# Weight conversion without clamp and magnitude, range checks moved to later blocks, in an attention and two-layer MoE kernel

## Chip, cores, metric

The kernel runs on one core of one Trainium2 chip. The metric is the time on the device in microseconds (us), the median of several executions; lower is better.

## What is computed

Three layers follow each other: a linear attention with a decay for each key row, a dense layer with a squared ReLU, and a layer of eight experts whose outputs are weighed by a matrix that is normalised eight times by rows and columns (Sinkhorn).

```python
# q, k, v, f_logit: (4, 8, 768, 48)
f = 1.0 / (1.0 + np.exp(-f_logit))
for t in range(S):
    state = f[:, :, t, :, None] * state + np.einsum('bhd,bhe->bhde', k[:, :, t], v[:, :, t])
    y[:, :, t] = np.einsum('bhd,bhde->bhe', q[:, :, t], state)

# x: (3072, 384), w_in: (384, 2048), w_out: (2048, 384)
r = np.maximum(x @ w_in, 0.0)
x = (r * r) @ w_out

# w_gate: (384, 8), w1: (8, 384, 1024), w2: (8, 1024, 384); P is N x 8
for e in range(E):
    h = np.maximum(x @ w1[e], 0.0)
    out += P[:, e:e + 1] * (h @ w2[e])
```

`w_in` and `w_out` are float64; the kernel reads their eight bytes as an int64 and makes a float32 of them itself.

## The kernel before

**Stages.** The 3072 tokens are eight blocks of 384 (NB = 8), each of three chunks of 128 (c = 0 to 23, three to a block). The dense layer goes block by block, and in each block over 16 slices of the hidden width (NF = 16). Step i = 16 * block + slice has a first product `e1` (`products_in`, L713 in block 0, L717 later), a ReLU `r` (L722) and a square `sq` (L725) on ScalarE, from block 1 on a rounding `hi` on ScalarE (L729) and a rest `lo` on VectorE (L733), and a second product `e2` (`m_out`, L742 in block 0, L746 later), two steps behind. From block 1 on each product is three matmuls with float32r parts. After the eight blocks come the experts (L983 and L1045).

**Attention of the next block** runs between the steps of the dense layer. For a chunk there are on TensorE `kt` (the transposed keys, L474), `sc` (scores, L459 or L453), `ds` (the state's increment, L499 or L492) and `mix` (the output, L537 and L546, from chunk 6 on L553); on VectorE two scans (`scanr` L400 to 402, `scanf` L407), the products `mulk` and `mulq` (L412, L416, later on GpSimd), the causal mask (L469, L464), the state (L507) and its decayed copy (L429). From chunk 6 on, a `mix` writes into the two PSUM banks of `e1`, so it waits for the ReLU of the step before it; the outputs leave by a ScalarE copy `yh` and a VectorE rest `yl` (L597, L595), and the next `e1` of that bank waits for them. When the three chunks of a block are done, `spread` (L603) moves rows inside the block's input by six DMAs; the block's first `e1` waits for these.

**Weight conversion.** For slice n, `ldw` loads 768 int64 values in each of 128 partitions. Class `F64` makes float32 of them: the magnitude of the high word (ScalarE, L1362), the low word scaled (ScalarE, L1365), a clamp of the magnitude to the float32 range (VectorE, L1370), the exponent and mantissa bits shifted (VectorE, L1375), the sign put in (VectorE, L1379), and the sum of both words (GpSimd, L1383). The result `R[n]` is what block 0 multiplies with. For block 1 and later it is split: `cvh` (ScalarE, L335) and `cvl` (VectorE, L338). Four raw buffers serve the 16 loads, so load n + 4 waits for the sum of n.

**Operands for the experts.** When a block's output `x2t` is there (L753), `xbs` (L875), `xbh` (ScalarE, L882) and `xbl` (L886) make sums of its rows, and `xbo` (L891) writes each of 15 operands to DRAM. Two buffers of the pool `rawp` hold them, and later the raw expert weights.

**The order.** All instructions are steps of a class `Plan`: engine, assumed duration, due time (in steps of the dense layer), needs, and an earliest start in microseconds. `Plan.order` lists the steps engine by engine in the order of an assumed schedule; each engine then runs its own list strictly in that order. The set `soft` holds steps that yield to others, the set `port` steps on VectorE and GpSimd that are not to overlap. SyncE's list is the order of all DMA issues, each assumed to take 0.48 us. `keep_warm` (L284) fills idle stretches of TensorE's assumed schedule in the first part with matmuls of no use.

```python
def load(self, name, kb, due, fn, needs=(), n=1, start=0.6, rate=350.0):
    self.add(name + ("issue",), "sp", 0.48 * n, due, fn, needs, start=start)
    self.add(name, "dma", kb / rate, due, lambda: None, [name + ("issue",)], lag=1.2)
```

**Ranges.** A flag says whether a general path has to run instead: `in_range` takes the least decay of all chunks (`minf`) and compares it with a bound. Weights outside the float32 range are clamped.

Of the kernel before, what the change touches and what calls it, by code (L numbers as in the profile page):

```python
# [28 lines left out]
NCH = B * NCB  # L29
# [50 lines left out]
class Plan:  # L80
# [15 lines left out]
    def add(self, name, eng, dur, due, fn, needs=(), lag=0.0, start=0.0):  # L96
        assert name not in self.steps, name
        self.steps[name] = (eng, dur, due, fn, [n for n in needs if n is not None], lag, start)

    def load(self, name, kb, due, fn, needs=(), n=1, start=0.6, rate=350.0):  # L100
        self.add(name + ("issue",), "sp", 0.48 * n, due, fn, needs, start=start)
        self.add(name, "dma", kb / rate, due, lambda: None, [name + ("issue",)], lag=1.2)

    def order(self):
# [75 lines left out]
def body(tc, fkq, v, wm, wa, wc, gate, seqs, out):  # L180
# [49 lines left out]
    def if_(ok, name):  # L230
        return name if ok else None
# [93 lines left out]
    def cv_abs(n):  # L325
        cvt[n] = cvp.tile([128, KD, TB // 2 + 1], F32, tag="t", name="cv_t")
        R[n] = wb.tile([128, WCOL], F32, tag=f"b{n}", name="r")
        F64(nc, cvt[n][:, :, 0:TB // 2], raws[n], R[n]).magnitude()

    def cv_total(n):  # L330
        F64(nc, cvt[n][:, :, 0:TB // 2], raws[n], R[n]).total(R[n])

    def cv_hi(n):
        new_w(n)
# [3 lines left out]
        dve.tensor_tensor(out=W[n][1], in0=R[n], in1=W[n][0].bitcast(F32), op=ALU.subtract)  # L338

    for n in range(NF):  # L340
        part = lambda m, n=n: getattr(F64(nc, cvt[n][:, :, 0:TB // 2], raws[n], R[n]), m)()
# [8 lines left out]
        plan.off_port |= {("cvb", n, 0), ("cvb", n, 1)}  # L350
# [248 lines left out]
    def spread(blk):  # L599
        X = x1[blk].bitcast(F32)  # L600
        for j in range(2):
            for k in range(KD):
                sp.dma_start(out=X[64 * j + DH:64 * j + 64, :, k, :], in_=X[64 * j + 16 * k:64 * j + 16 * k + 16, :, NP - 1, :])  # L603

    moved = []
    for c in range(NCH):
# [80 lines left out]
        else:  # L687
            at("yl", "none", 0, 3, lambda c: None, [("yh", c)])
        if q == CPB - 1 and blk:
            add(("sprd", blk), "sp", 3.0, g + to(3, 0.5), lambda blk=blk: spread(blk), [("yl", c - i) for i in range(CPB)], lag=2.2)  # L690

    def close_left():
        left.close()
# [194 lines left out]
    def xb_out(j, o):  # L888
        p, c = divmod(j, NB // NGRP)
        n = xb_at(j, o)  # L890
        sp.dma_start(out=xd[p, o][:, :, c * 128:(c + 1) * 128], in_=xb[j][:, n:n + 2])  # L891
# [197 lines left out]
    users += [("xb", j, [("xbo", j, o) for o in ROW_OPS]) for j in range(NB - 1)]  # L1089
    for g in range(NSTEP):  # L1090
        users += [("wa", g, [("w2lo", g, 0), ("w2lo", g, 1), ("wsum", g, 5)]), ("wc", g, [("w2lo", g, 2), ("w2lo", g, "c")])]
    slot_of = {}
    for n in range(2, len(users)):
        prev = users[n - 1]
        slot_of[users[n][:2]] = users[n - 2][2] + ([] if n == 2 else [("ld" + prev[0], prev[1], "issue")])

    for j in range(NB):
# [12 lines left out]
        for n, o in enumerate(ROW_OPS):  # L1110
            src = list(src0)
            m = SUMS.index(o) if o in ROW_SUM else 0
            if o in ROW_SUM and m >= (2 if mine else 1):
                src.append(("xbl", j, SUMS[m - (2 if mine else 1)]))
            if o in ROW_SUM and not mine:
                src.append(("xbl", j, ROW_OPS[n - 1]) if n else None)
            if o == 10:
                src += [("xbs", j, 2, len(ROW_SUM[2]) // 2 - 1)]
            if o == 5:
                src += [("xbs", j, 10, 0)]  # L1120
            for k in range(len(ROW_SUM.get(o, ())) // 2):
# [5 lines left out]
            add(("xbo", j, o, "issue"), "sp", 0.48, due(n) + 0.2, lambda j=j, o=o: xb_out(j, o), [("xbl", j, o)])  # L1127
# [221 lines left out]
class F64:  # L1349

    def __init__(self, nc, t, raw, flat=None):
        self.nc, self.t, self.flat = nc, t, flat
        self.high = raw.bitcast(I32).rearrange("p (n two) -> p n two", two=2)[:, :, 1]
        self.word = raw.bitcast(U32).rearrange("p (n two) -> p n two", two=2)[:, :, 0]

    def like(self, a):
        return a.rearrange("p (a b) -> p a b", a=KD) if self.flat is not None else a

    def magnitude(self):
        self.nc.scalar.activation(out=self.t, in_=self.like(self.high.bitcast(F32)), func=ACTF.Abs)  # L1362

    def low(self):
        self.nc.scalar.activation(out=self.word.bitcast(I32), in_=self.word, func=ACTF.Copy, scale=2.0 ** -29)  # L1365

    def clamp(self):
        dve, t = self.nc.vector, self.t
        out = t if self.flat is None else self.like(self.flat)
        dve.tensor_scalar(out=out, in0=t, scalar1=F64_LOW, scalar2=F64_HIGH, op0=ALU.max, op1=ALU.min)  # L1370

    def fields(self):
        dve, ti = self.nc.vector, self.t.bitcast(I32)
        src = ti if self.flat is None else self.like(self.flat.bitcast(I32))
        dve.tensor_scalar(out=ti, in0=src, scalar1=0x07FFFFFF, scalar2=3, op0=ALU.bitwise_and, op1=ALU.logical_shift_left)  # L1375

    def sign(self):
        dve, ti = self.nc.vector, self.t.bitcast(I32)
# [263 lines left out]
```

## Time and profile before

| | |
|---|---|
| runs | 1983.05, 1983.74, 1985.0 us; median 1983.74 |
| profiled execution | 1984.72 us, of which 1982.7 us are the span from the first to the last instruction |
| TensorE busy | 1964.8 us, 99% of the span |
| VectorE, ScalarE, GpSimd busy | 1399.0, 908.5, 972.4 us |
| mean granted TensorE clock | 0.998 |

The profile's page lists busy time by engine and by source line. Its other views are a timeline of one engine (with the idle time before an instruction, and what ended it), a table of busy time by stretches, the chain of work that ended last (followed back from the end), and groups of instructions by line. In those, a float32 matmul counts twice (two passes), so a slice's product of three such matmuls stands as x6, and one of nine float32r matmuls as x9.

### The profile page before, as it was taken

How to read it: one execution, taken by the hardware profiler on the slowest of the kernel's cores; microseconds unless marked ns; L12 is line 12 of the kernel's file. 1: busy time of each engine (PE TensorE's matmuls, PEld its weight loads, DVE VectorE, ACT ScalarE, POOL GpSimd, SP SyncE). 2: the span in 40 equal slices, each digit the busy share in tenths (PEclk: the TensorE clock that was granted, in tenths of full speed). 3: DMA queues.
4: the chain of work that ended last, by engine and by line, in shares of the span. 5: the costliest groups of instructions: out<-in, count | busy, mean ns of one | idle time of the engine just before them, and what ended most of it. 6: DMA issues, size and time to landing. Idle time of an engine off the chain costs nothing.

```text
span 1982.7 us, 29656 instructions
## 1 busy us (share of the span) xinstructions
PE 1964.8 (99%) x10921; PEld 1665.1 (84%) x10921; DVE 1399.0 (71%) x2314; ACT 908.5 (46%) x1643; POOL 972.4 (49%) x915
## 2 busy tenths in 40 slices
PE   8999999999999999999999999999999999999998
PEld 6699999999988888888888888888888888888887
DVE  8987666752577777666777777676677777766676
ACT  6665555655644443333444443433444444333342
POOL 2520111100245667776665556646666556666661
PEclk9999999999999999999999999999999999999999
DMA  7524343425202111121111114411111011111101
GB/s 267 179 77 115 106 111 100 111 70 188 79 33 66 49 53 58 59 67 48 57 33 48 33 49 161 142 32 57 33 55 49 32 48 33 56 40 48 40 24 50
DMA packets 102322, 146.61 MB, mean 74 GB/s; under 512 B 23608, under 2 KB 71320, under 8 KB 102168
## 3 DMA queue, kind: packets, MB, share of 16 engines
q1 hardware_dynamic: 102168, 144.63, 23.2%
q8 instruction: 88, 1.44, 0.3%
q14 instruction: 66, 0.54, 0.1%
HBM read 115.42 MB, written 21.14 MB: 69 GB/s over the span
## 4 chain that ended last, share of the span: by engine, by line
PE 94%; DVE 4%; issue 1%; DMA 1%; ACT 0%; SPq 0%; DVEq 0%; ACTq 0%
PE o L1045 40%; PE e L983 33%; PE a L746 8%; PE e L717 8%; PE a L742 1%; PE e L713 1%; PE y L553 1%; PE lg L761 1%; DVE sg L400 1%; PE pp L492 0%; PE pp L453 0%; PE ktr L474 0%; DVE QP L464 0%; DVE cv_t L1375 0%; DVE r L1370 0%
## 5 line engine op out<-in xcount | busy, mean ns | idle before, releaser
L1045 PE MATMUL o<-h,w 128*128 128x512 f32 x3456 | 790.7, 389 | 0.0
L1045 PEld LDWEIGHTS o<-h,w 128*128 128x128 f32 x3456 | 648.3, 188 | 135.0
L983 PE MATMUL e<-x,w 128*128 128x512 f32 x2304 | 536.2, 390 | 0.2 <-DVE vt L1010 0.2
L983 PEld LDWEIGHTS e<-x,w 128*128 128x128 f32 x2304 | 430.0, 188 | 94.5 <-DVE vt L1006 2.4
L1081 POOL TENSOR_TENSOR acc<-acc,sc 128x512 f32<-128x512 f32 x252 | 388.0, 1548 | 129.8 <-DVE sc L1072 126.6
L1072 DVE TENSOR_TENSOR sc<-o,pb 128x512 f32<-128x512 f32 x261 | 179.3, 687 | 213.6 <-PE o L1045 209.0
L934 ACT CAST w<-rawa 128x640 fp32r<-128x640 f32 x128 | 89.8, 726 | 285.3 <-DMA rawa<-in_wa_dram 142.7
L1010 DVE TENSOR_TENSOR v<-v,e 128x512 f32<-128x512 f32 x256 | 174.8, 683 | 64.5 <-PE e L983 57.8
L717 PE MATMUL e<-x,w 128*128 128x384 f32 x1008 | 193.5, 337 | 2.0 <-DMA x<-x 1.8
L934 ACT CAST w<-rawc 128x640 fp32r<-128x640 f32 (+1 forms) x128 | 97.2, 782 | 209.1 <-PE o L1045 157.9
L938 DVE TENSOR_TENSOR w<-rawa,w 128x640 fp32r<-128x640 f32 x128 | 152.6, 1211 | 57.2 <-ACT w L934 57.1
L1029 POOL TENSOR_TENSOR h<-vt,h 128x512 fp32r<-128x512 f32 x64 | 83.5, 1305 | 199.6 <-ACT vt L1024 197.4
L717 PEld LDWEIGHTS e<-x,w 128*128 128x128 f32 x1008 | 175.8, 188 | 3.8 <-ACT xb L882 2.0
L746 PE MATMUL a<-hi,w 128*128 128x384 f32 x672 | 173.9, 339 | 0.0
L1029 POOL TENSOR_TENSOR h<-v,h 128x512 fp32r<-128x512 f32 x64 | 82.8, 1295 | 154.3 <-ACT v L1024 77.7
L733 DVE TENSOR_TENSOR lo<-g,hi 128x384 fp32r<-128x384 f32 x112 | 74.9, 674 | 110.3 <-ACT hi L729 107.3
L1003 ACT ACTIVATE v<-e 128x512 f32<-128x512 f32 x128 | 76.3, 596 | 155.9 <-PE e L983 117.7
L1010 DVE TENSOR_TENSOR vk<-vk,e 128x512 f32<-128x512 f32 x192 | 131.8, 687 | 18.2 <-PE e L983 0.2
L983 PE MATMUL e<-xr,w 128*128 128x512 f32 x576 | 143.2, 392 | 0.1
L412 POOL TENSOR_TENSOR kq<-kq,sg 128x512 f32<-128x512 f32 x18 | 21.5, 1195 | 237.5 <-DVE sg L400 157.8
L983 PEld LDWEIGHTS e<-xr,w 128*128 128x128 f32 x576 | 106.9, 188 | 24.9 <-DVE v L1010 1.6
L938 DVE TENSOR_TENSOR w<-rawc,w 128x640 fp32r<-128x640 f32 (+1 forms) x128 | 120.8, 946 | 9.7 <-ACT w L934 9.5
(144 smaller groups left out, 2371.1 us busy)
## 6 DMA issues: line engine op xcount, KB each, us to landing
rawa<-in_wa_dram SPq DMA_DIRECT2D x64, 384.0 KB
rawc<-in_wc_dram SPq DMA_DIRECT2D x64, 384.0 KB
xd<-xb SPq DMA_DIRECT2D x120, 128.0 KB
raw<-in_wm_dram SPq DMA_DIRECT2D x16, 768.0 KB
x<-xd SPq DMA_DIRECT2D x24, 512.0 KB
pb<-ptd SPq DMA_DIRECT2D x16, 768.0 KB
kq<-in_fkq_dram SPq DMA_DIRECT2D x23, 512.0 KB
fraw<-in_fkq_dram SPq DMA_DIRECT2D x24, 256.0 KB
```

The costliest lines, as they stand in the source:

```text
L717: pe.matmul(ps, w[wl][:, k * 128:(k + 1) * 128], xx[:, xl, k, :], start=n == 0, stop=n == 3 * KD - 1)
L733: dve.tensor_tensor(out=lo, in0=g, in1=hi.bitcast(F32), op=ALU.subtract)
L746: pe.matmul(acc1[j][m], W[f][wl][:, D + m * 128:D + (m + 1) * 128], g, start=f == 0 and n == 0, stop=f == NF - 1 and n == 2)
L934: act.copy(out=W2[g, k][:, 0, 0:n], in_=src)
L938: dve.tensor_tensor(out=W2[g, k][:, 1, 0:n], in0=src, in1=W2[g, k][:, 0, 0:n].bitcast(F32), op=ALU.subtract)
L983: pe.matmul(bank[g, c], w[a], x[:, b], start=o == CHAIN[c][0] and n == 0, stop=n == 2, skip_group_check=True)
L1003: act.activation(out=t, in_=c, func=ACTF.Copy, scale=-1.0)
L1010: dve.tensor_tensor(out=t, in0=t, in1=c, op=op)
L1029: pool.tensor_tensor(out=h[:, 1], in0=hid_src(g, o), in1=h[:, 0].bitcast(F32), op=ALU.subtract)
L1045: pe.matmul(ob[q, t, m], w[:, a, c:c + 128], h[:, b], start=half == f == n == 0, stop=half == f == 1 and n == 2)
L1072: dve.tensor_tensor(out=dst, in0=ob[q, t, m], in1=pbt[p, e][:, t * TB:(t + 1) * TB], op=ALU.mult)
L1081: eng.tensor_tensor(out=acc[p, t, m], in0=acc[p, t, m], in1=sc[q, t, m], op=ALU.add)
```

## The change

1. The conversion drops the clamp (L1370) and the magnitude (L1362). One VectorE step `shifted` takes the high word itself: shift left by three, then a mask; the sign step, the low word and the sum stay.
2. The ranges are checked later: for blocks j = 1 to 4 four slices of the raw weights each are loaded a second time (`ldchk`, 768 KB) into a third kind of user of the two `rawp` buffers, while block j + 1 is worked on. For each slice ScalarE takes the magnitude of the high words, and VectorE reduces it to its largest and its least value. `in_range` combines the 32 values by six small steps and raises the flag if one lies outside.
3. Operands of block 0 (`xbs`, `xbh`, `xbl`) may start at an assumed 152 us at the earliest.
4. A DMA issue is assumed to take 0.64 us in place of 0.48, a `spread` 3.84 in place of 3.0.
5. A constant tile `span` of 3 x 16 float32 in each partition (192 bytes).

```diff
+XB0_AT = 152.0
-        self.add(name + ("issue",), "sp", 0.48 * n, due, fn, needs, start=start)
+        self.add(name + ("issue",), "sp", 0.64 * n, due, fn, needs, start=start)
+    span = const.tile([128, 3, NF], F32, name="span")
+    ends = span[:, 2, 0:2]
...
-        add(("cva", n), "act", 0.75, due, lambda n=n: cv_abs(n), [("ldw", n), if_(n >= 3, ("cvs", n - 3))], start=CV_AT + CV_STEP * n)
-        add(("cvw", n), "act", 0.74, due, lambda p=part: p("low"), [("ldw", n), ("cva", n)])
-        add(("cvb", n, 0), "dve", 0.88, due, lambda p=part: p("clamp"), [("cva", n)])
-        add(("cvb", n, 1), "dve", 0.88, due, lambda p=part: p("fields"), [("cvb", n, 0)])
-        add(("cvb", n, 2), "dve", 0.96, due, lambda p=part: p("sign"), [("cvb", n, 1)])
+        add(("cvw", n), "act", 0.9, due, lambda n=n: F64(nc, None, raws[n]).low(), [("ldw", n)], start=CV_AT + CV_STEP * n)
+        add(("cvb", n, 1), "dve", 0.93, due, lambda n=n: cv_shift(n), [("ldw", n), if_(n >= 3, ("cvs", n - 3))], start=CV_AT + CV_STEP * n)
+        add(("cvb", n, 2), "dve", 0.93, due, lambda n=n: fields(n).sign(), [("cvb", n, 1)])
...
+    SPAN_AT = {j: range(NF // 4 * (j - 1), NF // 4 * j) for j in range(1, 5)}
+    for j, group in SPAN_AT.items():
+        add(("ldspan", j, "issue"), "none", 0, (j + 1) * NF + 1, lambda j=j: span_new(j), slot_of["span", j])
+        prev = ("ldspan", j, "issue")
+        for k, n in enumerate(group):
+            d = (j + 1) * NF + 2.2 + 3.2 * k
+            plan.load(("ldchk", n), 786, d, lambda j=j, n=n: sp.dma_start(out=chk[j], in_=wm[n]), [prev])
+            for m, (key, eng) in enumerate(((0, "act"), (2, "dve"), (1, "dve"))):
+                plan.soft.add(("span", n, key))
+                add(("span", n, key), eng, 0.92, d + 1 + 0.1 * m, lambda j=j, n=n, key=key: span_of(j, n, key), [("ldchk", n) if m == 0 else ("span", n, 0 if m == 1 else 2)])
+            prev = ("span", n, 1)
...
-        soft = lambda name, eng, dur, d, fn, needs: (plan.soft.add(name), add(name, eng, dur, d, fn, needs))
+        soft = lambda name, eng, dur, d, fn, needs, start=0.0 if j else XB0_AT: (plan.soft.add(name), add(name, eng, dur, d, fn, needs, start=start))
...
-    add("range", "dve", 0.3, n1 - 12, in_range, [("scanf", NCH - 1)])
+    add("range", "dve", 1.0, n1 - 12, in_range, [("scanf", NCH - 1)] + [("span", n, 1) for n in range(NF)])
...
+    def shifted(self):
+        dve, ti = self.nc.vector, self.t.bitcast(I32)
+        dve.tensor_scalar(out=ti, in0=self.like(self.high), scalar1=3, scalar2=0x3FFFFFFF, op0=ALU.logical_shift_left, op1=ALU.bitwise_and)
+    def largest(self, out, least):
+        h = self.high.bitcast(F32)
+        self.nc.vector.tensor_reduce(out=least if out is None else out, in_=h, axis=AX.X, op=ALU.min if out is None else ALU.max)
```

The order changes with it. TensorE at the start of block 0, before: `e` is an `e1`, `a` an `e2` (three rows each), `warm` a matmul of no use, `ktr` chunk 3's transposed keys.

```order
L713 MATMUL e_459<-x_301,r 128x384 x3
L713 MATMUL e_471<-x_301,r 128x384 x3
L284 MATMUL warm<-shift 128x128 x2
L742 MATMUL a_493<-g,r 128x384
L742 MATMUL a_494<-g,r 128x384
L742 MATMUL a_495<-g,r 128x384
L713 MATMUL e_506<-x_301,r 128x384 x3
L474 MATMUL ktr<-shift,kq_117 128x128 x4
```

TensorE at the same place, with the change (the line numbers are three higher):

```order
L716 MATMUL e_458<-x_303,r 128x384 x3
L716 MATMUL e_470<-x_303,r 128x384 x3
L716 MATMUL e_483<-x_303,r 128x384 x3
L745 MATMUL a_494<-g,r 128x384
L745 MATMUL a_495<-g,r 128x384
L745 MATMUL a_496<-g,r 128x384
L716 MATMUL e_510<-x_303,r 128x384 x3
L477 MATMUL ktr<-shift,kq_118 128x128 x4
```

The third `e1` stands where the matmuls of no use stood, and a fourth `e1` comes ahead of the keys of chunk 3.

SyncE around the `spread` of block 2 (the six DMAs of `x` onto itself), before; `xd` are the experts' operands of block 0, `QP` and `vt` moves and loads for the attention:

```order
L891 DMA xd_14_134<-xb 256x1x128
L443 DMA QP_127<-kq_117 48x4x64 x2
L891 DMA xd_13_137<-xb 256x1x128
L443 DMA QP_127<-kq_117 48x4x64 x2
L891 DMA xd_11_138<-xb 256x1x128
L603 DMA x_1296<-x_1296 16x2x384 x6
L891 DMA xd_12_139<-xb 256x1x128
```

SyncE at the same place, with the change:

```order
L380 DMA fraw_116<-in_fkq_dram 128x512
L388 DMA vt_126<-in_v_dram 64x384 x2
L446 DMA QP_127<-kq_119 48x4x64 x2
L606 DMA x_1257<-x_1257 16x2x384 x6
L894 DMA xd_6_132<-xb 256x1x128
L894 DMA xd_7_133<-xb 256x1x128
```

All 15 operand writes of block 0 now stand behind the `spread`; before, eight of them stood ahead of it.

## Rows read from the trace of the kernel before

**Rows 1.** The page, busy time of the engines: us, share of the span, instructions.

```profile
PE 1964.8 (99%) x10921; PEld 1665.1 (84%) x10921; DVE 1399.0 (71%) x2314; ACT 908.5 (46%) x1643; POOL 972.4 (49%) x915
```

**Rows 2.** Timeline of TensorE: start, us, instruction, idle time before and its releaser.

```profile
28.62 4.11 PE L713 MATMUL e<-x,r 128*128 128x384 f32 x12
32.56 0.61 PE L284 MATMUL warm<-shift 128*128 128x128 f32 x4
33.61 2.20 PE L742 MATMUL a<-g,r 128*128 128x384 f32 x6 [0.45 <-ACT g L725]
...
39.24 0.66 PE L474 MATMUL ktr<-shift,kq 128*128 128x128 f32 x4 [1.49 <-DVE kq L412]
...
142.01 1.85 PE L717 MATMUL e<-x,w 128*128 128x384 f32 x9 [0.28 <-DVE x L595]
...
156.52 0.44 PE L746 MATMUL a<-lo,w 128*128 128x384 f32 x1 [0.94 <-DVE lo L733]
...
168.39 2.57 PE L717 MATMUL e<-x,w 128*128 128x384 f32 x9 [1.75 <-DMA x<-x]
...
204.52 1.03 PE L553 MATMUL y<-QP,vt 128*64 128x64 f32 x28 [0.63 <-ACT g L722]
...
266.24 1.03 PE L553 MATMUL y<-QP,vt 128*64 128x64 f32 x28 [0.94 <-ACT g L722]
```

**Rows 3.** Chain that ended last, around block 2's first product: start, us, what.

```profile
166.15 2.15 DMA x<-x
...
170.96 2.44 PE a L746 x9
173.40 1.56 PE e L717 x9
```

**Rows 4.** Stretch of 1 us: busy of PE, PEld, DVE, ACT, POOL; clock; DMA share; GB/s.

```profile
170.00:171.00 1.00, 1.00 (x5) 1.00 (x4) 0.63 (x2) 0.00 (x1) 0.29 (x1) 0.50 0.25 74
```

**Rows 5.** Instruction groups, 20 to 110 us: busy us, mean ns, idle before.

```profile
L1383 POOL TENSOR_TENSOR r<-cv_t,raw 128x768 int32<-128x768 int32 x16 | 35.4, 2222 | 53.6 <-DMA vt<-in_v_dram 22.6 <-DVE cv_t L1379 13.2 <-DVE d L399 4.6
...
L1370 DVE TENSOR_SCALAR r<-cv_t 128x768 f32<-128x768 f32 x16 | 15.1, 944 | 0.6 <-ACT cv_t L1362 0.6
```

**Rows 6.** Timeline of VectorE in block 0's first steps.

```profile
21.10 0.95 DVE L1370 TENSOR_SCALAR r<-cv_t 128x768 f32<-128x768 f32 x1
...
30.82 0.95 DVE L1379 SCALAR_TENSOR_TENSOR cv_t<-raw,cv_t 128x768 int32<-128x768 int32 x1
...
38.50 0.68 DVE L412 TENSOR_TENSOR kq<-kq,sg 128x512 f32<-128x512 f32 x1
```

**Rows 7.** Timeline of SyncE's DMA issues (start, us for all of the row's issues).

```profile
30.22 18.37 SPq L323 DMA_DIRECT2D raw<-in_wm_dram  x5
...
163.53 0.57 SPq L891 DMA_DIRECT2D xd<-xb  x1
164.19 3.82 SPq L603 DMA_DIRECT2D x<-x  x6
...
285.34 3.81 SPq L603 DMA_DIRECT2D x<-x  x6
```

**Rows 8.** Timeline of TensorE, last chunk of block 3's attention and the next first product.

```profile
281.42 1.15 PE L553 MATMUL y<-QP,vt 128*64 128x64 f32 x32
...
293.07 1.72 PE L717 MATMUL e<-x,w 128*128 128x384 f32 x9
```

**Rows 9.** VectorE's reductions, groups of the whole span.

```profile
L1403 DVE TENSOR_REDUCE sk_mx<-L 128x1 f32<-128x192 f32 x1 | 0.4, 353 | 0.0
...
L1328 DVE TENSOR_REDUCE mx<-minf 128x1 f32<-128x8 f32 x1 | 0.2, 160 | 0.0
```

**Rows 10.** Timeline of ScalarE: a load waited for, and a wait ahead of a ReLU.

```profile
36.16 0.92 ACT L1362 ACTIVATE cv_t<-raw 128x768 f32<-128x768 f32 x1 [1.66 <-DMA raw<-in_wm_dram]
...
203.78 0.30 ACT L882 CAST xb<-xb 128x128 fp32r<-128x128 f32 x1 [2.82 <-DVE xb L875]
```

**Rows 11.** Busy of PE, PEld, DVE, ACT, POOL in 50 us of block 3.

```profile
250.00:300.00 50.00, 49.06 (x532) 47.62 (x531) 33.81 (x79) 27.03 (x60) 7.49 (x6) 1.00 0.39 105
```

More of the change, by code (lines that the diff above doesn't have):

```diff
@@ L323, in ldw, with fields, cv_shift, cv_total @@
         sp.dma_start(out=raws[n], in_=wm[n])
-    def cv_abs(n):
+    def fields(n):
+        return F64(nc, cvt[n][:, :, 0:TB // 2], raws[n], KD)
+    def cv_shift(n):
         cvt[n] = cvp.tile([128, KD, TB // 2 + 1], F32, tag="t", name="cv_t")
+        fields(n).shifted()
+    def cv_total(n):
         R[n] = wb.tile([128, WCOL], F32, tag=f"b{n}", name="r")
-        F64(nc, cvt[n][:, :, 0:TB // 2], raws[n], R[n]).magnitude()
-    def cv_total(n):
-        F64(nc, cvt[n][:, :, 0:TB // 2], raws[n], R[n]).total(R[n])
+        fields(n).total(R[n])
     def cv_hi(n):
@@ L340, in body @@
     for n in range(NF):
-        part = lambda m, n=n: getattr(F64(nc, cvt[n][:, :, 0:TB // 2], raws[n], R[n]), m)()
         due = n - LEAD_W
         plan.load(("ldw", n), 786, LOADS["w"] + n if n < 4 else due - 3, lambda n=n: ldw(n), [if_(before(n) >= 0, ("cvs", before(n)))], start=W_AT)
-        add(("cva", n), "act", 0.75, due, lambda n=n: cv_abs(n), [("ldw", n), if_(n >= 3, ("cvs", n - 3))], start=CV_AT + CV_STEP * n)
-        add(("cvw", n), "act", 0.74, due, lambda p=part: p("low"), [("ldw", n), ("cva", n)])
-        add(("cvb", n, 0), "dve", 0.88, due, lambda p=part: p("clamp"), [("cva", n)])
-        add(("cvb", n, 1), "dve", 0.88, due, lambda p=part: p("fields"), [("cvb", n, 0)])
-        add(("cvb", n, 2), "dve", 0.96, due, lambda p=part: p("sign"), [("cvb", n, 1)])
+        add(("cvw", n), "act", 0.9, due, lambda n=n: F64(nc, None, raws[n]).low(), [("ldw", n)], start=CV_AT + CV_STEP * n)
+        add(("cvb", n, 1), "dve", 0.93, due, lambda n=n: cv_shift(n), [("ldw", n), if_(n >= 3, ("cvs", n - 3))], start=CV_AT + CV_STEP * n)
+        add(("cvb", n, 2), "dve", 0.93, due, lambda n=n: fields(n).sign(), [("cvb", n, 1)])
         add(("cvs", n), "pool", 1.95, due, lambda n=n: cv_total(n), [("cvb", n, 2), ("cvw", n)])
-        plan.off_port |= {("cvb", n, 0), ("cvb", n, 1)}
+        plan.off_port.add(("cvb", n, 1))
         gone = [(s, k) for k in left_by(n) for s in ("e2", "cvl")]
@@ L689, in body @@
         if q == CPB - 1 and blk:
-            add(("sprd", blk), "sp", 3.0, g + to(3, 0.5), lambda blk=blk: spread(blk), [("yl", c - i) for i in range(CPB)], lag=2.2)
+            add(("sprd", blk), "sp", 3.84, g + to(3, 0.5), lambda blk=blk: spread(blk), [("yl", c - i) for i in range(CPB)], lag=2.2)
     def close_left():
@@ L1086, in body @@
     last_pe = None
+    SPAN_AT = {j: range(NF // 4 * (j - 1), NF // 4 * j) for j in range(1, 5)}
     users = [("cv", n, [("cvs", n)]) for n in late[-2:]]
-    users += [("xb", j, [("xbo", j, o) for o in ROW_OPS]) for j in range(NB - 1)]
+    for j in range(NB - 1):
+        users.append(("xb", j, [("xbo", j, o) for o in ROW_OPS]))
+        if j in SPAN_AT:
+            users.append(("span", j, [("span", n, 1) for n in SPAN_AT[j]]))
     for g in range(NSTEP):
@@ L1095, in body, with span_new, span_of @@
         slot_of[users[n][:2]] = users[n - 2][2] + ([] if n == 2 else [("ld" + prev[0], prev[1], "issue")])
+    chk = {}
+    def span_new(j):
+        chk[j] = rawp.tile([128, WCOL], I64, tag="raw", name="chk")
+    def span_of(j, n, k):
+        w = F64(nc, None, chk[j])
+        if k == 0:
+            w.magnitude(w.high.bitcast(F32))
+        elif k == 1:
+            w.largest(None, span[:, 1, n:n + 1])
+        else:
+            w.largest(span[:, 0, n:n + 1], None)
+    for j, group in SPAN_AT.items():
[8 more added lines that the diff above has]
+            prev = ("span", n, 1)
     for j in range(NB):
@@ L1126, in body @@
             soft(("xbl", j, o), eng, 0.2 if mine else 0.5, due(n) + 0.1, lambda j=j, o=o: xb_lo(j, o), [("xbh", j, o)])
-            add(("xbo", j, o, "issue"), "sp", 0.48, due(n) + 0.2, lambda j=j, o=o: xb_out(j, o), [("xbl", j, o)])
+            add(("xbo", j, o, "issue"), "sp", 0.64, due(n) + 0.2, lambda j=j, o=o: xb_out(j, o), [("xbl", j, o)])
             add(("xbo", j, o), "dma", 0.4, due(n) + 0.2, lambda: None, [("xbo", j, o, "issue")], 2.8)
@@ L1329, in in_range @@
         dve.tensor_scalar(out=mx, in0=mx, scalar1=MIN_DECAY, scalar2=None, op0=ALU.is_lt)
+        dve.tensor_reduce(out=ends[:, 0:1], in_=span[:, 0], axis=AX.X, op=ALU.max)
+        dve.tensor_reduce(out=ends[:, 1:2], in_=span[:, 1], axis=AX.X, op=ALU.min)
+        dve.tensor_scalar(out=ends[:, 0:1], in0=ends[:, 0:1], scalar1=F64_HIGH, scalar2=None, op0=ALU.is_gt)
+        dve.tensor_scalar(out=ends[:, 1:2], in0=ends[:, 1:2], scalar1=F64_LOW, scalar2=None, op0=ALU.is_lt)
+        dve.tensor_tensor(out=mx, in0=mx, in1=ends[:, 0:1], op=ALU.max)
+        dve.tensor_tensor(out=mx, in0=mx, in1=ends[:, 1:2], op=ALU.max)
     def in_range_all():
@@ L1349, with __init__ @@
 class F64:
-    def __init__(self, nc, t, raw, flat=None):
-        self.nc, self.t, self.flat = nc, t, flat
+    def __init__(self, nc, t, raw, parts=None):
+        self.nc, self.t, self.parts = nc, t, parts
         self.high = raw.bitcast(I32).rearrange("p (n two) -> p n two", two=2)[:, :, 1]
@@ L1358, in like, with magnitude @@
     def like(self, a):
-        return a.rearrange("p (a b) -> p a b", a=KD) if self.flat is not None else a
-    def magnitude(self):
-        self.nc.scalar.activation(out=self.t, in_=self.like(self.high.bitcast(F32)), func=ACTF.Abs)
+        return a if self.parts is None else a.rearrange("p (a b) -> p a b", a=self.parts)
+    def magnitude(self, out=None):
+        self.nc.scalar.activation(out=self.t if out is None else out, in_=self.high.bitcast(F32), func=ACTF.Abs)
     def low(self):
@@ L1368, in clamp @@
         dve, t = self.nc.vector, self.t
-        out = t if self.flat is None else self.like(self.flat)
-        dve.tensor_scalar(out=out, in0=t, scalar1=F64_LOW, scalar2=F64_HIGH, op0=ALU.max, op1=ALU.min)
+        dve.tensor_scalar(out=t, in0=t, scalar1=F64_LOW, scalar2=F64_HIGH, op0=ALU.max, op1=ALU.min)
     def fields(self):
         dve, ti = self.nc.vector, self.t.bitcast(I32)
-        src = ti if self.flat is None else self.like(self.flat.bitcast(I32))
-        dve.tensor_scalar(out=ti, in0=src, scalar1=0x07FFFFFF, scalar2=3, op0=ALU.bitwise_and, op1=ALU.logical_shift_left)
+        dve.tensor_scalar(out=ti, in0=ti, scalar1=0x07FFFFFF, scalar2=3, op0=ALU.bitwise_and, op1=ALU.logical_shift_left)
+    def shifted(self):
+        dve, ti = self.nc.vector, self.t.bitcast(I32)
+        dve.tensor_scalar(out=ti, in0=self.like(self.high), scalar1=3, scalar2=0x3FFFFFFF, op0=ALU.logical_shift_left, op1=ALU.bitwise_and)
     def sign(self):
```

## The prediction

> **What bounds the kernel now.** I read the page's busy times first: TensorE is busy for 1964.8 of 1982.7 us, 99% [rows 1]. So a part of the change pays only where TensorE stands idle, runs something useless, or runs at a low clock, and the next view is TensorE's timeline, read for the idle time in square brackets. From block 0's first product, at 28.62 us, on there are seven such places before the experts [rows 2]: two in block 0 (0.45 and 1.49 us, with 0.61 us of warm matmuls just before), three in block 1 (0.28, 0.94, 1.75 us) and two later (0.63 and 0.94 us). [...] The rest of the span is TensorE's own work, which the change leaves alone: its order differs in blocks 0 and 1 only.
>
> **The change, part by part.**
>
> *Conversion.* Sixteen clamps of 0.944 us leave VectorE, 15.1 us in all, and the new shift takes the place of the old one; I price both alike [rows 5], though the new one reads every second word: the sign step reads the same words and took 0.95 us [rows 6]. Between 39.24 and 142.01 us TensorE has no such bracket [rows 2], so most of the 15.1 us only makes room. It is on the path in one place, the first steps of block 0.
> The attention ahead of it stays: at 21.10 us two conversion steps follow the state, in either order (clamp and shift before, shift and sign now), and the mask comes after them. So the first product still starts near 28.62 us; I allow 0.2 us either way.
> The third `e1` needs the sum of slice 2. Its sign step began at 30.82 us [rows 6]; with the clamps of slices 0 to 3 gone and the shift of slice 3 now ahead of it, three steps fewer stand there, and it begins near 30.82 - 3 x 0.95 = 28.0 us. The sign then ends at 28.9 and the sum, 2.22 us [rows 5], at 31.1 us; a microsecond of waits on the way leaves it in time. Two `e1` end at 32.56 us, where the warm matmuls began [rows 2]; the third fits without a gap, and 0.61 + 0.45 us go.
> The keys of chunk 3 need `mulk`, which began at 38.50 us [rows 6]. Up to it 14 conversion steps become 10, so it begins near 38.5 - 4 x 0.95 = 34.7 us. TensorE reaches the keys after four `e1` and one `e2`, at 28.62 + 5 x 1.97 = 38.5 us (1.97 is half of the two `e1`'s 32.56 - 28.62): over 3 us of slack, and the 1.49 us go. Term: **-2.5 us** (ends: -3 with an earlier start; -1 if a load of raw weights is late, since slice 5 came only 36.16 - 30.22 = 5.9 us after its issue [rows 7, 10]).
> The sixteen magnitudes of ScalarE (0.92 us each, as the one in rows 10) leave a stretch in which it was the releaser of one wait, 0.45 us, counted above.
>
> *Operands of block 0 later.* The chain behind the 1.75 us is: an operand write blocks SyncE until 163.53, the `spread` is issued from 164.19 for 3.82 us [rows 7], its DMA takes 2.15 us [rows 3], and block 2's first product waits. With the change no operand write stands ahead of the `spread`, and TensorE runs `mix` two `e2` earlier, with three `e1` and three `e2` between it and block 2's first product. That is block 3's order already, which had no wait: its last `mix` ended at 281.42 + 1.15 = 282.57, its `spread` was issued from 285.34 for 3.81 us [rows 7], so even the last of the six landed at 289.15 + 2.15 = 291.3, and the product started at 293.07 us [rows 8], 1.8 us later. So I take out 1.75 + 1.89, and the 0.94 us before it, which waited for a `lo` of the `e2` that now comes after `mix`. The 0.28 us may stay. Term: **-4.6 us** (ends: -0.9 if the `spread` is still late, -4.9).
>
> *Range checks.* Each of 16 slices brings a 768 KB load, a magnitude of 0.92 us on ScalarE and two reductions on VectorE. No reduction of 768 stands in the trace; by the rows of 192 and 8 elements, 353 and 160 ns [rows 9], an element costs 193 / 184 = 1.05 ns, so 768 cost 0.160 + 760 x 0.00105 = 0.96 us (ends: 0.35 and, by two operands at 1.0 us, 1.0). Per block of 60 us that is 8 x 0.96 = 7.7 us of VectorE and 3.7 us of ScalarE. In 50 us of block 3 VectorE had 16.2 and ScalarE 23.0 us free [rows 11]: on average there is room. What can be late is single steps. `mix` waits for the ReLU of the step before, with one `e2` (1.56 us) between; ScalarE's list is strict, so anything ahead of that ReLU that waits, delays `mix`: the 0.63 us came from an operand's rounding that waited 2.82 us for VectorE [rows 10]. The change puts magnitudes that wait for a load of up to 5.9 us at such places, and takes the roundings away at the two that stalled. There are 12 such `mix` in blocks 2 to 5. I count on three to four stalls of 0.63 to 0.94 us in place of two: 2.6 against 1.57 us. Term: **+1.0 us** (ends: -1.6 with none; +7.8 with 0.78 us at all twelve, 9.4 - 1.6).
>
> *The rest, at nothing.* DMA traffic rises by 12.6 MB over some 240 us, 50 GB/s beside 105 [rows 11]. The six small steps of `in_range` (0.16 us each, as the last of rows 9) run late in the dense layer, where TensorE had no gap; if that cover is missing they cost 1 us. The longer issue times are the planner's only. 192 bytes of constants shift addresses: no row prices that, I take 0.
>
> **Sum.** -2.5 - 4.6 + 1.0 = -6.1 us. Against the profiled execution, 1984.72, that is 1978.6; this execution was 0.98 us above the median of the runs, 1983.74, from which I forecast **1977.6 us**.
>
> **Rivals.**
>
> 1. *Nothing new stalls.* The two old stalls go as well: 1983.74 - 2.5 - 4.9 - 1.6 = 1974.7. For it: no rounding stands ahead of those two ReLUs any more. Against: a load of 768 KB waited for by a strict list. Chance 0.12.
> 2. *The checks give the gain back.* Stalls at nine of the twelve `mix`: 9 x 0.78 - 1.6 = +5.4 in place of +1.0, so 1982.0; at all twelve 1984.4. For it: VectorE rises from 34 to some 40 of 50 us there. Chance 0.16.
> 3. *The spread of block 1 is still late*, because the scans and `lo` ahead of the last `yl` take the time that the operands took: 1.75 + 1.89 stay, 1981.2. Against: the same order in block 3. Chance 0.08.
> 4. *Slower: a check's load stands ahead of a block's spread in the DMA rings.* The spread's 2.15 us become up to the 5.9 us of the raw load, 3.75 more; beyond the 1.8 us of slack it decides. TensorE would wait 1.95 us, and after 1.75 the clock fell, so 1.9 us more each: 4 x 3.85 = 15.4 us, 1983.74 - 7.1 + 15.4 = 1992.0. Against: the new order has several issues between the last check of a block and the spread. Chance 0.06.
>
> [...]
>
> **Chances.** The forecast, 1975.5 to 1979.7, has 0.58. A difference of 0.2%, 4 us, is about what a measurement of this kernel can tell from none, so faster means below 1979.8: the forecast and rival 1, 0.58 + 0.12 = 0.70; slower means above 1987.7: 0.06; within: rivals 2 and 3, 0.24. The range runs from rival 1, 1974.5, into rival 2, 1984.0; it leaves out rival 4 and the ends of the first and second, together under 0.2.
>
> **What would show it.** After the change TensorE's timeline should have no bracket of 0.4 us or more from 28.6 to 170 us, no warm matmul after the first `e1`, and a granted clock of 1.00 around 170 us; the logits of block 0 (at 113 us before) should start 2 to 3 us earlier, those of block 1 (at 181 us) 6 to 8 us earlier, and those of block 5 (at 425 us) 5 to 8 us earlier, the difference being what blocks 2 to 5 give back. The reductions should read 0.9 to 1.0 us. I am wrong if block 0 starts later, if a wait for `x<-x` comes back at any block's first product, or if ReLUs behind magnitudes hold up more than four `mix`.

## The result: slower by 0.6%, in the stage that the change leaves alone

The changed kernel took **1996.35 us** (median of 5 runs, 1995.34 to 1999.19); the kernel before, in runs beside it, 1984.78. The ratio is 1.0061, with a 95% interval of 1.0047 to 1.0076. The forecast was 1977.6 us with a range up to 1984.0: wrong, and on the other side. The profiled execution has a span of 1994.6 us against 1982.7, so 11.9 us more, at a granted clock of 0.999.

Up to the experts the change wins about what was forecast, 5.5 us of 6.1. These are rows of TensorE's timeline after the change (start, us, instruction, idle time before), beside which [rows 2] stand:

```profile
28.91 6.04 PE L716 MATMUL e<-x,r 128*128 128x384 f32 x18
34.79 2.10 PE L745 MATMUL a<-g,r 128*128 128x384 f32 x6
...
39.62 1.16 PE L462 MATMUL pp<-kq 48*128 48x128 f32 x16 [0.36 <-DVE kq L419]
...
110.95 2.07 PE L764 MATMUL lg<-gate_sb,x2t 128*128 128x8 f32 x18
...
170.98 0.62 PE L749 MATMUL a<-hi,w 128*128 128x384 f32 x2 [0.60 <-ACT x2t L756]
...
172.66 0.62 PE L749 MATMUL a<-hi,w 128*128 128x384 f32 x2 [0.35 <-ACT x2t L756]
...
174.85 2.07 PE L764 MATMUL lg<-gate_sb,x2t 128*128 128x8 f32 x18
...
274.13 1.03 PE L556 MATMUL y<-QP,vt 128*64 128x64 f32 x28 [0.22 <-ACT g L725]
...
396.79 1.03 PE L556 MATMUL y<-QP,vt 128*64 128x64 f32 x28 [0.55 <-ACT g L725]
...
524.50 2.11 PE L764 MATMUL lg<-gate_sb,x2t 128*128 128x8 f32 x16 [0.42 <-ACT x2t L756]
```

Three `e1` run in one piece, with no warm matmul and no wait behind them. The keys of chunk 3, which waited 1.49 us, run at 38.66 us without a wait; the scores behind them (L462) wait 0.36 us for `mulq`. No wait for `x<-x` is left at block 2's first product, near 168 us. The logits of the same three blocks before:

```profile
113.31 2.07 PE L761 MATMUL lg<-gate_sb,x2t 128*128 128x8 f32 x18
...
181.04 2.07 PE L761 MATMUL lg<-gate_sb,x2t 128*128 128x8 f32 x18
...
529.98 2.11 PE L761 MATMUL lg<-gate_sb,x2t 128*128 128x8 f32 x16 [0.40 <-ACT x2t L753]
```

So block 0's start 2.4 us earlier, block 1's 6.2 and the last block's 5.5.

All of it and more is lost behind that point. The page's instruction groups (busy us, mean ns of one, idle before) show the experts' matmuls: the second products with the hidden tiles `h`, and the first products, which take twelve of their fifteen operands `x` from the left of each partition and three, `xr`, from the right. The kernel before:

```profile
L1045 PE MATMUL o<-h,w 128*128 128x512 f32 x3456 | 790.7, 389 | 0.0
...
L983 PE MATMUL e<-x,w 128*128 128x512 f32 x2304 | 536.2, 390 | 0.2 <-DVE vt L1010 0.2
...
L983 PE MATMUL e<-xr,w 128*128 128x512 f32 x576 | 143.2, 392 | 0.1
```

The changed kernel, with the busy times of the engines ahead (for [rows 1]):

```profile
PE 1981.0 (99%) x10919; PEld 1668.6 (84%) x10919; DVE 1421.7 (71%) x2336; ACT 908.8 (46%) x1643; POOL 977.0 (49%) x915
...
L1048 PE MATMUL o<-h,w 128*128 128x512 f32 x3456 | 804.5, 394 | 0.0
...
L986 PE MATMUL e<-x,w 128*128 128x512 f32 x2304 | 537.8, 391 | 0.3 <-DVE vt L1009 0.2
...
L986 PE MATMUL e<-xr,w 128*128 128x512 f32 x576 | 145.2, 396 | 0.1
```

The same 3456 second products, in the same order, with no idle time ahead of them in either kernel, took 13.8 us more; the first products 1.6 and 2.0 us more. Together 17.4 us, and 17.4 - 5.5 = 11.9 us is the difference of the spans. No wait shows it, since nothing waits: each matmul simply takes longer. In the timeline it is a run of 108 second products that grows. Before, from one such run to what follows it 24.47 us pass:

```profile
1320.80 24.64 PE L1045 MATMUL o<-h,w 128*128 128x512 f32 x108
1345.27 8.34 PE L983 MATMUL e<-x,w 128*128 128x512 f32 x36
```

and after, 25.20 us:

```profile
1325.79 25.36 PE L1048 MATMUL o<-h,w 128*128 128x512 f32 x108
1350.99 8.36 PE L986 MATMUL e<-x,w 128*128 128x512 f32 x36
```

By the trace's starts, neighbouring second products stood 226.9 ns apart before (mean over the 3411 that are followed by another one within 300 ns) and 230.8 ns after. What changed for them is where their operands lie. Line 203 puts `span`, 192 bytes, into the constants; these lie first on the left of each partition, so the weights (`wpool`), the raw buffers and the operands `x` on the left all move up by 192 bytes, while the hidden tiles `h` and the operand `xr`, in pools of the right side, stay. The traces hold no addresses; these are from the built programs. Before, the first weight buffer began at byte 4832 and the first hidden tile at 167904: both leave 224 when divided by 256. After the change the weights leave 160.

### The profile page after: what moved, and what is told of

It is laid out like the page before. It is cut to its first block, busy times and chain, and to the rows that moved or that the text cites. A ratio compares the mean times of both kernels' runs of the same rounds, so it can differ in the third digit from the quotient of the medians.

```text
span 1994.6 us, 29716 instructions
## 1 busy us (share of the span) xinstructions
PE 1981.0 (99%) x10919; PEld 1668.6 (84%) x10919; DVE 1421.7 (71%) x2336; ACT 908.8 (46%) x1643; POOL 977.0 (49%) x915
## 4 chain that ended last, share of the span: by engine, by line
PE 94%; DVE 3%; DMA 1%; ACT 1%; issue 1%; SPq 0%; DVEq 0%; ACTq 0%
PE o L1048 40%; PE e L986 33%; PE a L749 7%; PE e L720 7%; PE a L745 1%; PE e L716 1%; PE y L556 1%; PE lg L764 1%; DMA chk<-in_wm_dram 1%; PE pp L495 0%; PE ktr L477 0%; DVE QP L467 0%; PE pp L456 0%; DMA raw<-in_wm_dram 0%; PE pp L462 0%
## 5 line engine op out<-in xcount | busy, mean ns | idle before, releaser
L1048 PE MATMUL o<-h,w 128*128 128x512 f32 x3456 | 804.5, 394 | 0.0
L986 PE MATMUL e<-x,w 128*128 128x512 f32 x2304 | 537.8, 391 | 0.3 <-DVE vt L1009 0.2
L720 PE MATMUL e<-x,w 128*128 128x384 f32 x1008 | 193.2, 338 | 0.2
L986 PE MATMUL e<-xr,w 128*128 128x512 f32 x576 | 145.2, 396 | 0.1
L736 DVE TENSOR_TENSOR lo<-g,hi 128x384 fp32r<-128x384 f32 x112 | 70.4, 632 | 98.8 <-ACT hi L732 97.3
L941 DVE TENSOR_TENSOR w<-rawc,w 128x640 fp32r<-128x640 f32 (+1 forms) x128 | 124.8, 977 | 9.4 <-ACT w L937 9.2
```

Source lines behind the costliest of these rows:

```text
L720: pe.matmul(ps, w[wl][:, k * 128:(k + 1) * 128], xx[:, xl, k, :], start=n == 0, stop=n == 3 * KD - 1)
L736: dve.tensor_tensor(out=lo, in0=g, in1=hi.bitcast(F32), op=ALU.subtract)
L941: dve.tensor_tensor(out=W2[g, k][:, 1, 0:n], in0=src, in1=W2[g, k][:, 0, 0:n].bitcast(F32), op=ALU.subtract)
L986: pe.matmul(bank[g, c], w[a], x[:, b], start=o == CHAIN[c][0] and n == 0, stop=n == 2, skip_group_check=True)
L1048: pe.matmul(ob[q, t, m], w[:, a, c:c + 128], h[:, b], start=half == f == n == 0, stop=half == f == 1 and n == 2)
```

## Experiments

The theory after the comparison (A): a matmul whose moving operand and whose weights stand differently to each other slows down. Its rivals: (B) only the place of the weights counts; (C) addresses don't count, and another part of the change slows the experts, such as the two raw buffers that swapped places, or the added loads.

### The address, alone and taken out

**e1**, the change with its constants laid into the tile `P`, which is idle until the ranges have been reduced:

```diff
-    span = const.tile([128, 3, NF], F32, name="span")
+    span = P[:, 0:3 * NF // NE, :].rearrange("p (k a) e -> p k (a e)", k=3)
```

> The changed kernel with its 192 bytes of constants laid into tile P, which is idle until after the ranges have been reduced: every engine issues what it issues in the changed kernel, and every buffer lies where it lay before. A, a shift of one side's buffers against the other side's slows the second expert products: about 1978 us (the 5.4 us that the profile of the change had won at the first expert product, 1983.7 - 5.4), the groups of 108 second products 24.49 us each again. B, only where the weights themselves lie counts: the same 1978 us. C, addresses don't count and the expert stage is slower for another part of the change (its loads, its order, the two raw buffers that swapped): still 1996 us and 24.7 to 25.2 us a group.

Measured: 1979.76 us, ratio 0.9981 (0.9972 to 0.9990). The page's groups:

```profile
PE 1963.7 (99%) x10919; PEld 1663.3 (84%) x10919; DVE 1418.2 (72%) x2336; ACT 909.3 (46%) x1643; POOL 977.4 (49%) x915
...
L1048 PE MATMUL o<-h,w 128*128 128x512 f32 x3456 | 790.5, 389 | 0.0
```

The second products are back at 790.5 us. C falls: with every instruction of the change in place, and in the same order on every engine, the 192 bytes alone make the difference between 0.9981 and 1.0061, 0.8% or 15.9 us.

**e2**, the change with 64 bytes on the other side, so that the two sides stand to each other as before modulo 256:

```diff
+    ctx.enter_context(tc.tile_pool(name="fill", bufs=1, side="right")).tile([128, 16], F32, name="fill")
     x1e = ctx.enter_context(tc.tile_pool(name="x1e", bufs=1, side="right", reuse_waits="tile"))
```

> The changed kernel with 64 unused bytes ahead of the buffers on the right, so that left (192 up) and right (64 down) differ by 256 bytes from before, and weights, operands and hidden tiles stand to each other as before modulo 128. A, the offset of one side against the other: about 1978 us, second products 227 ns apart. B, where the weights lie: still 1996 us, second products 230 to 233 ns apart. C, not the addresses: 1996 us.

Measured: 1980.71 us, ratio 0.9981 (0.9972 to 0.9990); second products 790.5 us, 226.8 ns apart. The weights lie where the changed kernel has them, and it is as fast as e1: B falls.

**e3** and **e4**, the kernel before with nothing but a shift:

```diff
     flag = const.tile([128, 1], I32, name="flag")
+    const.tile([128, 48], F32, name="fill")
```

is e3, with 192 bytes on the left; e4 has the `fill` pool of e2, with 64 bytes on the right.

> The kernel before with an unused constant of 192 bytes and nothing else. A and B: about 2001 us (1983.7 and the 17 us that the expert stage of the changed kernel lost). C: 1984 us.

> The kernel before with 64 unused bytes ahead of the buffers on the right and nothing else: the weights stay where they were, the hidden tiles move. A: 1996 to 2001 us, second products 230 to 233 ns apart. B and C: 1984 us and 227 ns.

Measured: e3 2002.25 us, ratio 1.0089 (1.0074 to 1.0105); e4 2012.64 us, 1.0141 (1.0125 to 1.0156). e3 is the loss of the change without the change. In e4 the weights didn't move at all, and it is the slower of the two, beyond the 2001 us expected; its row of the page:

```profile
L1046 PE MATMUL o<-h,w 128*128 128x512 f32 x3456 | 813.0, 395 | 0.0
```

### Which pair of operands

**e9** moves the hidden tiles alone, **e10** the hidden tiles and the weights:

```diff
+        new("fill1", 1, side="right").tile([128, 16], F32, name="fill1")
         pools["h"] = new("h2p", 1, side="right")
+        new("fill2", 1, side="right").tile([128, 48], F32, name="fill2")
```

and for e10, besides, the 192 bytes of e3 ahead of `wpool` and 64 bytes behind it:

```diff
+    ctx.enter_context(tc.tile_pool(name="fill4", bufs=1)).tile([128, 16], F32, name="fill4")
     rawp = ctx.enter_context(tc.tile_pool(name="rawp", bufs=2))
```

> The kernel before with the hidden tiles of the expert stage alone 64 bytes lower (64 unused bytes ahead of them, 192 behind, so that what follows moves by 256). If hidden tile against weights is the pair that counts: second products 233 ns apart, the first products as before (227.7, and 228.7 with xr), 1984.3 + 3456 x 6.5 ns = 2007 us. Rival, one whole side against the other (results, other engines' tiles): 226.9 ns and 1984 us.

> The kernel before with the weights alone 192 bytes up and the hidden tiles alone 64 bytes down; everything else stays or moves by 256. If operand against weights is the pair: second products 226.9 ns again (their two sides are 256 apart), and the first products, whose x now stands 192 off its weights, slower for the first time, 230 to 232 ns: 1984.3 + 2880 x 2.5 to 4.5 ns = 1991 to 1997 us. Rival, a shift of the weights or of the hidden tiles is bad by itself: second products 230 to 233 ns and 2000 us or more, first products as they were.

Measured: e9 2007.27 us, as worked out ahead; e10 1989.62 us (one run each). The page of e9:

```profile
L1047 PE MATMUL o<-h,w 128*128 128x512 f32 x3456 | 812.9, 394 | 0.0
...
L985 PE MATMUL e<-x,w 128*128 128x512 f32 x2304 | 536.7, 390 | 0.1
...
L985 PE MATMUL e<-xr,w 128*128 128x512 f32 x576 | 143.1, 392 | 0.2 <-DVE v L1012 0.2
```

The page of e10:

```profile
L1049 PE MATMUL o<-h,w 128*128 128x512 f32 x3456 | 791.3, 390 | 0.0
...
L987 PE MATMUL e<-x,w 128*128 128x512 f32 x2304 | 542.0, 393 | 0.1
...
L987 PE MATMUL e<-xr,w 128*128 128x512 f32 x576 | 143.6, 393 | 0.1
```

In e9 the second products alone are slow. In e10, where hidden tiles and weights have both moved but stand to each other as before modulo 256, they are fast again, and the first products with `x`, whose weights moved away from them, are slow for the first time: 5.8 us, 2.5 ns each. The time is a little below the 1991 to 1997 us expected, because the 576 products with `xr`, whose weights moved away from them by the same 192 bytes, took only 0.4 us more, where they take 2.0 us more in e3 and in the changed kernel. So for the hidden tiles the pair of moving operand and weights is shown; a whole side against the other, or one address by itself, is not what counts. For `x` it fits; for `xr` something besides the pair must count, and what, wasn't tried.

### How far apart matters

**e5**, **e6** and **e16** are e4 with 128, 192 and 32 bytes.

> The kernel before with 128 unused bytes ahead of the buffers on the right: hidden tiles and weights stand to each other as before modulo 128, but not modulo 256. If the offset counts modulo 128: 1984 us, second products 226.9 ns apart. If it counts modulo 256 or more: slower, as in the run with 64 bytes (2012 us, 233 ns) or somewhere between.

> The kernel before with 192 unused bytes ahead of the buffers on the right: the same offset modulo 128 and 256 as in the run with 64 bytes less 128, and as in the changed kernel modulo 512, with the weights left where they were. If only the offset of one side against the other counts: 230 to 232 ns between second products and 1997 to 2002 us, as with 192 bytes on the left. If which side moves counts too: 233 ns and 2012 us, as with 64 bytes on the right.

> The kernel before with 32 unused bytes ahead of the buffers on the right. If any offset that is no multiple of 256 bytes costs: second products 230 to 234 ns apart and 1996 to 2012 us. If 32 bytes are within what is read at once for both: 226.9 ns and 1984 us.

Measured, one run each: 2010.68, 1995.64 and 2008.37 us. All address runs together, ordered by how far `h` lies below its weights, counted from the kernel before (busy us from the pages, ns from one start to the next in the traces, bytes modulo 256 by the built programs):

| `h` against weights, bytes | kernel | second products, us | ns apart | first with `x` / `xr`, us | time, us |
|---|---|---|---|---|---|
| 0 | before | 790.7 | 226.9 | 536.2 / 143.2 | 1984.4 |
| 0 | e1 (the change) | 790.5 | 226.8 | 536.6 / 143.0 | 1979.8 |
| 32 | e16 | 813.0 | 233.3 | 536.2 / 145.6 | 2008.4 |
| 64 | e4 | 813.0 | 233.3 | 538.3 / 145.5 | 2012.6 |
| 64 | e9 (`h` alone) | 812.9 | 233.3 | 536.7 / 143.1 | 2007.3 |
| 128 | e5 | 811.0 | 232.7 | 538.9 / 145.1 | 2010.7 |
| 192 | e6 | 800.8 | 229.8 | 536.9 / 145.0 | 1995.6 |
| 192 | e3 | 807.4 | 231.7 | 537.3 / 145.2 | 2002.3 |
| 192 | the change | 804.5 | 230.8 | 537.8 / 145.2 | 1996.4 |
| 256 | e2 (the change) | 790.5 | 226.8 | 536.5 / 143.0 | 1980.7 |
| 256 | e10 | 791.3 | 227.0 | 542.0 / 143.6 | 1989.6 |

128 bytes are no better than 64, 256 are as good as 0, and 32 already cost the whole. At 192 the price is smaller and not the same in three kernels; e3 and e6 run the same instructions at the same offset and differ by 1.9 ns a product, so something besides this offset counts a little there. The first products with `x` also took 2 to 3 us more in e4 and e5, where `x` and its weights stood as before. What causes this wasn't tried.

### The parts of the change, at unmoved addresses

With the addresses out of the way (e1), the change is worth -0.19%. Its parts: the conversion stands in all the following kernels; the start of block 0's operands, the range checks and the issue costs are in or out, in all eight combinations. The edits, as far as a kernel has them, back to the kernel before:

```diff
-XB0_AT = 152.0
+XB0_AT = 0.0
...
-    SPAN_AT = {j: range(NF // 4 * (j - 1), NF // 4 * j) for j in range(1, 5)}
+    SPAN_AT = {}
...
-        self.add(name + ("issue",), "sp", 0.64 * n, due, fn, needs, start=start)
+        self.add(name + ("issue",), "sp", 0.48 * n, due, fn, needs, start=start)
```

(without checks, the six steps in `in_range` go too; the issue costs go back at all three places).

> The changed kernel with its constants in P and block 0's operands again without the start time. By the prediction's term this gives back 4.6 us: about 1984 to 1985 us, with TensorE waiting some 1.7 us for block 1's x near 168 us and a stretch at the granted clock 0.50 behind it. Rival, the later operands only moved the wait and the other terms won the 4 us: 1980 to 1981 us and no such wait.

> The changed kernel with its constants in P and without the range checks of blocks 2 to 5 (it leaves out those checks: 16 loads, 16 magnitudes, 32 reductions and the six steps at their end). By the prediction's term it gains 1.0 us: about 1978.8 us. By the profile of the change, in which the lead over before falls from 7.4 us at block 3's logits to 5.5 us at the last block's, it gains up to 1.9 us: 1977.9 us. Rival, the checks cost nothing: 1979.8 us.

> The kernel before with the conversion of the change alone: no clamp and no magnitude, and no check of the ranges in their place (it leaves the check of the weights' range out), block 0's operands and the issue costs as before, no new constants. By the prediction's term, 2.5 us of the stalls before block 0's first products: 1981.8 us. Rival, the stalls only wait elsewhere (a g at the end of block 1, block 1's x): 1984 us.

> The changed kernel with its constants in P and the old costs of SP's issues in the planner. The prediction put them at nothing: 1979.8 us. Rival, the spread or a load is issued too early again and block 1's x comes late: 1981 to 1984 us.

> Conversion and range checks, without the later operands and the issue costs, constants in P. By the prediction's term for the checks, +1.0 us on the conversion alone: 1979.7 us. Rival, the checks change only the order and hide wholly: 1978.7 us. If the order falls otherwise with every part: anywhere from 1977 to 1983 us, with other waits for g and x than in the conversion alone.

> Conversion and later operands of block 0, without range checks (left out) and the issue costs, constants in P. By the prediction's term, 4.6 us less than the conversion alone: 1974.1 us. Rival, with the conversion alone block 1's x was no longer late (its trace has no such wait), so there is nothing to win: 1978.7 us or, with another order, up to 1983 us.

> Conversion and the issue costs, without range checks (left out) and later operands, constants in P. By the prediction, which had this at nothing: 1978.7 us. If the order falls otherwise with every part: 1977 to 1983 us.

| run | operands later | checks | issue costs | time, us | ratio to before (95%) |
|---|---|---|---|---|---|
| e11 | | | | 1978.70 | 0.9971 (0.9961 to 0.9982) |
| e14 | x | | | 1978.70 | 0.9972 (0.9962 to 0.9983) |
| e13 | | x | | 1980.80 | 0.9987 (0.9978 to 0.9996) |
| e15 | | | x | 1981.56 | 0.9988 (0.9979 to 0.9997) |
| e12 | x | x | | 1982.33 | 0.9989 (0.9980 to 0.9998) |
| e8 | x | | x | 1982.12 | 0.9989 (0.9980 to 0.9998) |
| e7 | | x | x | 1982.56 | 0.9993 (0.9984 to 1.0002) |
| e1 | x | x | x | 1979.76 | 0.9981 (0.9972 to 0.9990) |

The conversion alone gives 5.8 us (0.29%; by its interval 3.6 to 7.7), not the 1 to 3 of its term. TensorE's timeline of e11 has no wait for `x<-x` near 168 us (the input of block 2, moved while block 1 is worked on; the expectations call it block 1's x) and few others:

```profile
150.95 0.34 PE L556 MATMUL y<-QP,vt 128*64 128x64 f32 x4
151.45 1.03 PE L556 MATMUL y<-QP,vt 128*64 128x64 f32 x28 [0.17 <-ACT g L725]
...
197.73 1.03 PE L556 MATMUL y<-QP,vt 128*64 128x64 f32 x28 [0.96 <-ACT g L725]
...
259.45 1.04 PE L556 MATMUL y<-QP,vt 128*64 128x64 f32 x28 [0.93 <-ACT g L725]
```

and in SyncE's timeline of the same kernel this `spread` is issued at 156.29 us, where [rows 7] have it at 164.19:

```profile
156.29 3.82 SPq L606 DMA_DIRECT2D x<-x  x6
```

The `mix` ahead of it runs at 150.95 us, before the change at 157.95. So the planner, given the new conversion, already writes the order that I had put down to the later operands. Averaged over the four pairs of kernels that differ in one part, the later operands give 0.4 us, the checks cost 1.5 and the issue costs 1.6 us. Each of these is a mean over four differences of kernels whose own intervals are 0.1% (2 us) to either side, so the first isn't told from zero, and the other two barely.

The parts don't add up, either: with any one of the three taken out of the whole the ratio is 1.6 to 2.4 us higher (e7, e8, e12 against e1; the intervals overlap), and none of them alone made e11 faster. The planner writes another order each time. In e8, without the checks, the waits for a ReLU at `mix` that the change had removed are back in TensorE's timeline:

```profile
200.18 1.03 PE L556 MATMUL y<-QP,vt 128*64 128x64 f32 x28 [0.63 <-ACT g L725]
...
261.89 1.04 PE L556 MATMUL y<-QP,vt 128*64 128x64 f32 x28 [0.94 <-ACT g L725]
...
323.14 1.03 PE L556 MATMUL y<-QP,vt 128*64 128x64 f32 x28 [0.63 <-ACT g L725]
...
384.54 1.03 PE L556 MATMUL y<-QP,vt 128*64 128x64 f32 x28 [0.65 <-ACT g L725]
```

So taking work away brought waits back, in the order that the planner writes without the checks; that these waits make up the difference of e8 to e1 is not shown, since e11 has such waits too and is faster. A version that does all that the change does and beats both kernels is e1, or e2: 0.9981 of the kernel before.

## Why the prediction was wrong, step by step

*What bounds the kernel.* The failed sentence is "The rest of the span is TensorE's own work, which the change leaves alone". The order of the experts' 6336 products was left alone; their speed was not. (The list of seven waits also leaves out an eighth, 0.40 us ahead of the last logits; it stayed, at 0.42.)

*The rest, at nothing.* The step that decided: "192 bytes of constants shift addresses: no row prices that, I take 0". It measured +15.9 us (e1 against the changed kernel), +0.9% when put into the kernel before (e3). A zero for want of a row was also given no end in the range, and no rival: that, more than the value, put the result outside. The rows that would have carried a bound were on the page: 3456 + 2304 + 576 products, busy for 1470 us, of which each 0.1% is 1.5 us. The longer issue costs, also at nothing, came to some 1.6 us in the planner's order, barely told from zero. As for the addresses, moving the hidden tiles alone by 64 bytes (e9) took the second products from 226.9 to 233.3 ns and the kernel from 1984 to 2007 us. Why the chip is slower there no run here shows.

*Conversion, -2.5.* At block 0 it came out: the first product at 28.91 us (28.6 was forecast), the third `e1` without a gap, the logits 2.4 us earlier. One step was off and hidden by its slack: `mulk` began at 37.01 us, not at 34.7, and the keys ran at 38.66. The shift cost what the old one did, 948 ns against 950. As a term it was mis-sized, since it also changed the order of block 1: 5.8 us alone.

*Operands later, -4.6.* The term's 1.89 us is what the two products behind the wait took longer: 2.57 us [rows 2] and 2.44 us, where the next took 1.56 [rows 3], with the granted clock at 0.50 [rows 4]. The wait for `x<-x` and the low clock behind it went (1.00 from 169 to 174 us in the changed kernel), and block 1's logits came 6.2 us earlier, as said. But the cause was wrong: without this part (e7, e11) they went too. Averaged over the combinations the part gives 0.4 us, not told from zero. Nor was it free of a new wait: in the changed kernel two casts of operands stand ahead of the copy of `x2t` for which TensorE waits 0.60 us at 170.98. ScalarE's timeline there:

```profile
170.03 0.52 ACT L885 CAST xb<-xb 128x128 fp32r<-128x128 f32 x2
170.46 0.85 ACT L756 COPY x2t<-a 128x384 f32<-128x384 f32 x2
```

All six kernels with the later operands have this wait, of 0.60 to 1.28 us near 171 us; the four with the new conversion but without them (e7, e11, e13, e15) have none.

*Range checks, +1.0.* The size agrees with the average over the combinations, 1.5 us, which is itself uncertain by about as much; the way it was worked out does not hold. The reductions took 948 ns, where 960 were worked out from [rows 9]:

```profile
L1428 DVE TENSOR_REDUCE span<-chk 128x1 f32<-128x768 f32 x32 | 30.1, 948 | 7.6 <-ACT chk L1400 7.6
```

VectorE's busy time in 250 to 300 us rose from 33.8 us [rows 11] to 38.5 (40 was said):

```profile
250.00:300.00 50.00, 49.71 (x458) 48.48 (x457) 38.51 (x90) 31.51 (x68) 7.74 (x6) 1.00 0.52 154
```

The three to four stalls at `mix`, 2.6 us, did not come: the changed kernel has two, 0.22 us at 274.13 and 0.55 at 396.79, less than the 1.57 us before. Where the checks cost their time is open.

*Rivals.* The fourth, the only one on the slow side, did not happen: no first product waits for `x<-x` in the changed kernel. By the trace's landings two spreads of the changed kernel took longer: block 3's, issued from 216.29 us, 3.1 us behind a check's load (4.3 us for its first move, 2.15 for its last), and block 4's, issued from 277.51 us, 0.6 us behind a load of `kq` and 9.4 us behind a check's (4.4 and 3.1 us); the moves of blocks 2, 5, 6 and 7 took 2.1 to 2.2 us each. TensorE waited for none of them. Without the shift of addresses, e1's 1979.8 us lies in the range, between the forecast's 1977.6 and the second rival's 1982.0. That is luck in part: the forecast's terms were -2.5, -4.6, +1.0 and 0, the measured ones -5.8, -0.4, +1.5 and +1.6.

## What to carry to other kernels

A tile allocated ahead of others moves every buffer behind it: before adding one, compare where TensorE's moving operand and its weights start, modulo 256 bytes here (32 bytes of offset cost 6.4 ns a product in e16), and keep that with a filler or by laying the new bytes into a tile that is idle (e1, e2). In a kernel that is bound by one engine, its own work is a term as well: count times mean ns of the largest group, looked at before any wait. And where a planner writes the order, a part's worth is not the wait that it was meant for; only runs with the part in and out, in more than one surrounding, tell it.

## What the runs showed of the hardware

A 128x128 by 128x512 product with the hidden tiles took 226.8 to 227.0 ns from start to start where operand and weights began at the same byte modulo 256. Where the operand lay 32, 64 or 128 bytes lower, modulo 256, it took 233.3, 233.3 and 232.7 ns, and at 192 bytes 229.8 to 231.7. That is up to 2.9% of the rate of an engine that is busy for 99% of the span, with no wait and no change of the granted clock (0.998 to 0.999 in the profiles of all these runs) to show for it. The products of the dense layers with 384 columns felt less: counting starts less than 200 ns apart, those with weights on the left stood 173.6 ns apart before and 173.4 in the changed kernel; by the page the 1008 first products from block 1 on were busy for 193.5 us before, 193.2 in the changed kernel and 194.4 in e4.
